# Second stage's down projection in seven block products, its weights' sums made in stage 1 and parked in device memory

## The chip, the cores and the metric

One core of a Trainium2 chip runs the whole kernel. The metric is device time in microseconds (us) of one execution. Engines are named as in the profile: PE (TensorE matmul), PEld (its weight load), DVE (VectorE), ACT (ScalarE), POOL (GpSimd), SP (SyncE, which issues nearly all DMAs here).

## The reference

Windowed attention, a gated feed-forward layer (stage 1) and a second feed-forward layer with a squared ReLU (stage 2). The change touches stage 2 and the preparation of its weights.

```python
attn = _attn_ref(q, k, v)                  # 4 x 8 heads, 576 tokens, window 64
x = heads side by side                     # 2304 tokens x 512
xn = x / rms(x) * rms_g                    # stage 1, d_ff = 1536
x = (silu(xn @ w_gate) * (xn @ w_val)) @ w_out
h = x @ w_in                               # stage 2, d_ff = 2048
out = (maximum(h, 0) ** 2) @ w_out2
```

## The kernel before

**Precision.** Every float32 operand of a product is kept as a high and a low part (`h`, `l`, type fp32r). A product of two of them is three matmuls for each 128 rows of contraction: high by high, low weight by high input, high weight by low input. The split of an operand is a cast on ACT or DVE (the high part) and a subtraction on DVE or POOL (the low part).

**Order.** Nothing is issued as it is written. `Schedule` collects steps, each with an engine (or two to choose from), a cost, the buffers that it reads and writes and a rank, and `issue` lays them out engine by engine in a simulated order; `LAG` is the delay that it assumes from a step's end to the start of a step on another engine. The engines then run their lists strictly in that order, with semaphores for the dependencies.

**Stage 1** (attention and the gated layer) decodes its weights on ACT and DVE (`decode`, L529 to L554). Beside it run 16 *jobs*, which prepare the weights of stage 2: `park_up(p)` and `park_down(p)` for each of 8 pairs p of 128-wide blocks of d_ff. A job decodes two blocks, splits them and writes them to device memory (`su`, `sd`). `park_up` also makes the four weight sums that the up projection's seven products need; `park_down` writes its two blocks as they are.

**Stage 2** works on 4 token blocks q of 576 tokens (two halves j of 288) and 8 pairs p, two pairs (`PG`) to a group. Tokens go in two halves of two q each (`HALVES`); in each half the 4 groups follow each other, and in a group the 2 token blocks. `operands(q)` makes the seven input blocks from `acc`. `up2` makes one unit (q, p): seven products of 6 matmuls of 128x128 weights by 288 columns (L766), taken from PSUM by copies (L771) and additions (L772), then the squared ReLU (L797) and the split (L804, L227). `down2` then makes, for each of 4 blocks c of 128 output columns and 2 halves j, one product over both pairs: 4 contraction blocks, 12 matmuls (`mm3`, L584, L586, L588). The running sum lies in `acc`: before the product ACT copies it into the PSUM bank (L823), after it ACT or DVE copies the bank back (L225).

```python
def down2(ds, acts, q, first, last):
    for c in range(KC):
        for j in range(2):
...
                if not first:
...
                    sc.add("act", c_act(PN), lambda b=b, pre=pre: nc.scalar.copy(ps[b][:, :PN], pre), ...)
                pe(12 * len(ds) // 2 * c_mm(PN), mm, ...)
```

The down weights have three buffers (`d0` to `d2`), the up weights two, the activations of two units six buffers of which four are in use.

## Time and profile before

| | |
|---|---|
| time, median of 3 runs | 939.1 us (938.45 to 939.8) |
| the profiled execution: time, span | 938.64 us, 936.9 us |
| busy, share of the span: PE, PEld | 98%, 92% |
| busy: DVE, ACT, POOL | 65%, 58%, 4% |
| granted TensorE clock, mean | 1.000 |
| stage 1's gated layer without attention, then stage 2 | about 125 to 551 us, 551 to 933 us |
| last matmul's end to the span's end | 3.6 us |

The time of an execution lies 1.7 us above its span. Busy shares are means over stages; PE's busy time holds its modelled pipeline, so a full row means that matmuls follow each other without a gap, not that the array is at its peak. Matmuls of 288 columns start one every 133 ns though each is shown with some 295 ns, since they overlap.

### The profile page before, as it was taken

How to read it: one execution, taken by the hardware profiler on the slowest of the kernel's cores; microseconds unless marked ns; L12 is line 12 of the kernel's file. 1: busy time of each engine (PE TensorE's matmuls, PEld its weight loads, DVE VectorE, ACT ScalarE, POOL GpSimd, SP SyncE). 2: the span in 40 equal slices, each digit the busy share in tenths (PEclk: the TensorE clock that was granted, in tenths of full speed). 3: DMA queues.
4: the chain of work that ended last, by engine and by line, in shares of the span. 5: the costliest groups of instructions: out<-in, count | busy, mean ns of one | idle time of the engine just before them, and what ended most of it. 6: DMA issues, size and time to landing. Idle time of an engine off the chain costs nothing.

```text
span 936.9 us, 17182 instructions
## 1 busy us (share of the span) xinstructions
PE 920.5 (98%) x6786; PEld 864.0 (92%) x6786; DVE 612.4 (65%) x1325; ACT 541.9 (58%) x1318; POOL 42.1 (4%) x48
## 2 busy tenths in 40 slices
PE   7989999999999999999999999999999999999998
PEld 6778899889988988988988999999999999999998
DVE  6999997789989978889996374333347333323340
ACT  5887884465565656565653364455567534555554
POOL 1000000001000101010211000000000000000000
PEclk9999999999999999999999999999999999999999
DMA  8664730334624523524646042242425352424212
GB/s 252 217 204 140 221 99 6 121 134 167 226 73 150 206 113 125 200 91 169 213 152 230 1 169 80 79 169 80 169 80 200 129 189 79 172 77 169 80 58 89
DMA packets 48001, 130.62 MB, mean 139 GB/s; under 512 B 5936, under 2 KB 22320, under 8 KB 43824
## 3 DMA queue, kind: packets, MB, share of 16 engines
q1 hardware_dynamic: 47392, 129.39, 40.0%
q8 instruction: 53, 0.87, 0.4%
q14 instruction: 28, 0.23, 0.1%
q10 hardware_dynamic: 528, 0.13, 0.1%
HBM read 101.71 MB, written 27.79 MB: 138 GB/s over the span
## 4 chain that ended last, share of the span: by engine, by line
PE 88%; DVE 9%; DMA 1%; ACT 0%; issue 0%; SPq 0%; DVEq 0%; ACTq 0%
PE ps L584 22%; PE ps L586 22%; PE ps L588 22%; PE ps L766 19%; DVE sm L422 2%; DVE R L226 1%; DMA k<-kT 1%; DVE xw L482 1%; PE ps L417 1%; PE ps L440 1%; DVE acc L445 1%; DVE Q L540 0%; DVE Q L539 0%; PE ps L907 0%; PE ps L430 0%; DVE pt L225 0%
## 5 line engine op out<-in xcount | busy, mean ns | idle before, releaser
L766 PE MATMUL ps<-R 128*128 128x288 f32 x1344 | 187.8, 295 | 0.0
L225 ACT COPY acc<-ps 128x288 f32<-128x288 f32 (+4 forms) x217 | 93.0, 431 | 160.3 <-PE ps L588 159.5
L766 PEld LDWEIGHTS ps<-R 128*128 128x128 f32 x1344 | 181.7, 188 | 0.1
L586 PE MATMUL ps<-L,R 128*128 128x288 f32 (+3 forms) x520 | 119.3, 322 | 0.0
L584 PE MATMUL ps<-L,R 128*128 128x288 f32 (+3 forms) x520 | 119.3, 322 | 0.0
L588 PE MATMUL ps<-L,R 128*128 128x288 f32 (+3 forms) x520 | 119.1, 321 | 0.0
L772 DVE TENSOR_TENSOR Q<-ps,Q 128x288 f32<-128x288 f32 x64 | 29.0, 454 | 117.6 <-ACT Q L771 106.7
L584 PE MATMUL ps<-R 128*128 128x256 f32 (+4 forms) x452 | 102.6, 347 | 0.8 <-ACT R L225 0.7
L586 PE MATMUL ps<-R 128*128 128x256 f32 (+4 forms) x452 | 100.5, 343 | 0.0
L588 PE MATMUL ps<-R 128*128 128x256 f32 (+4 forms) x452 | 100.3, 342 | 0.0
L797 DVE SCALAR_TENSOR_TENSOR Q<-Q 128x576 f32<-128x576 f32 x62 | 47.9, 773 | 72.3 <-ACT Q L771 71.3
L588 PEld LDWEIGHTS ps<-L,R 128*128 128x128 f32 x520 | 85.5, 188 | 4.2
L586 PEld LDWEIGHTS ps<-L,R 128*128 128x128 f32 x520 | 85.5, 188 | 4.2
L584 PEld LDWEIGHTS ps<-L,R 128*128 128x128 f32 x520 | 85.3, 188 | 4.2
L584 PEld LDWEIGHTS ps<-R 128*128 128x128 f32 x452 | 77.0, 188 | 9.0 <-ACT R L225 1.0
L586 PEld LDWEIGHTS ps<-R 128*128 128x128 f32 x452 | 77.4, 189 | 7.0
L588 PEld LDWEIGHTS ps<-R 128*128 128x128 f32 x452 | 77.4, 189 | 7.0
L771 ACT COPY Q<-ps 128x288 f32<-128x288 f32 x128 | 51.1, 400 | 46.0 <-PE ps L766 44.6
L225 ACT CAST L<-Q 128x512 fp32r<-128x512 f32 (+3 forms) x81 | 45.8, 573 | 54.8 <-DVE Q L627 50.3
L227 DVE TENSOR_TENSOR L<-Q,L 128x576 fp32r<-128x576 f32 (+2 forms) x90 | 66.0, 742 | 10.8 <-ACT L L804 9.8
L424 ACT ACTIVATE sm<-sm,nb 128x128 f32<-128x128 f32 (+1 forms) x144 | 55.7, 392 | 17.5 <-DVE nb L422 16.6
L657 ACT COPY ps<-acc 128x512 f32<-128x512 f32 (+2 forms) x101 | 55.1, 550 | 16.2 <-DVE acc L225 15.0
(105 smaller groups left out, 1471.6 us busy)
## 6 DMA issues: line engine op xcount, KB each, us to landing
Q<-w SPq DMA_DIRECT2D x68, 512.0 KB, 4.6
R<-su SPq DMA_DIRECT2D x16, 1792.0 KB, 7.2
su<-L SPq DMA_DIRECT2D x24, 512.0 KB, 4.6
R<-sd SPq DMA_DIRECT2D x11, 1024.0 KB, 5.2
v<-vw SPq DMA_DIRECT2D x36, 256.0 KB, 3.6
sd<-L SPq DMA_DIRECT2D x16, 512.0 KB, 5.3
L<-sd SPq DMA_DIRECT2D x5, 1024.0 KB, 4.9
q<-qT SPq DMA_DIRECT2D x36, 128.0 KB, 3.2
```

What stands on the lines that cost most here:

```text
L225: copy = lambda e, out, in_: nc.scalar.copy(out, in_) if e == "act" else nc.vector.tensor_copy(out, in_)
L227: two = lambda e, out, a, b, op: (nc.vector if e == "dve" else nc.gpsimd).tensor_tensor(out, a, b, op=op)
L422: at("dve", 0.21, lambda p=p, i=i_, j=j: nc.vector.tensor_tensor_reduce(out=T[sm][:, p, :nk], in0=s_ps[j][:, i, :nk], in1=T["mask"][:, P - ...
L424: at("act", 0.39, lambda p=p: nc.scalar.activation(T[sm][:, p, :nk], T[sm][:, p, :nk], AF.Exp, bias=T[nb][:, p : p + 1], scale=-1.0, accum ...
L584: nc.tensor.matmul(acc, wh, xh, start=(i == 0 and not seeded), stop=False, skip_group_check=seeded)
L586: nc.tensor.matmul(acc, wl, xh, start=False, stop=False, skip_group_check=seeded)
L588: nc.tensor.matmul(acc, wh, xl, start=False, stop=(i == n - 1), skip_group_check=seeded)
L657: add("act", c_act(n), lambda b=b, dst=dst: nc.scalar.copy(ps[b][:, :n], dst), r=keys("acc", c, t), w=[("ps", b)])
L766: nc.tensor.matmul(bank, w_, x_, start=(start and i == 0), stop=(i == len(terms) - 1), skip_group_check=True)
L771: take = lambda src, k, dst, kd: act(lambda: nc.scalar.copy(dst(), src), [k], [kd])
L772: plus = lambda src, k, other, s, j: sc.add("dve", c_dve(PN), lambda: nc.vector.tensor_tensor(e(s, j), src, T[other], op=ALU.add), r=[k, o ...
L797: nc.vector.scalar_tensor_tensor(T[s], T[s], 0.0, T[s], op0=ALU.max, op1=ALU.mult)
```

## The change

`down2` takes the form that `up2` has. Two blocks of output columns (of 128, from the two halves of 256), two blocks of d_ff rows and two token halves make a 2 by 2 block product, done as seven products and sums of weights and activations in place of eight. Two such chains (k = 0, 1) cover 512 output columns, each product over both pairs (6 matmuls). `park_down` now makes four weight sums and writes seven blocks, as `park_up` does (`park_pair`). `up2` makes, from the squared ReLU of its four blocks, three more differences (R1 to R4 with the in-place ones) and splits seven blocks in place of four, as two pieces of 5 and 2 blocks (1440 and 576 columns). The running sum is no longer copied into PSUM: VectorE adds the bank to `acc` in place. `operands` also makes its differences in place in `acc`. A load of weights comes in two parts, each waited for by itself; the down weights have two buffers, the activations one set of two (a second for the last block). The planner's assumed delay is 0.25 in place of 0.4 from the stage-1 jobs on, and the stage-1 weights lie in other slots (`PLACE`).

```diff
-PLACE = [1, 7, 8, 2, 3, 4, 5, 6, 0]
+PLACE = [5, 6, 7, 1, 2, 3, 4, 8, 0]
...
-            EXTRA[:] = 0.09, 0.1
+            EXTRA[:] = 0.09, 0.1, 0.25
...
-    make(dr, [NPAIR, P, 2, 2, WE], F32, "sd")
+    make(dr, [NPAIR, P, 2, 7 * 256], F32, "sd")
...
+    def park_pair(z, p, srcs, swap):
+        f = decode(srcs, after=closed2)
...
+        one(1, a21, a22, ALU.add, fk[2] + fk[3])
+        one(0, lambda: q(1), a11, ALU.subtract, [("q", 1)] + fk[0])
+        one(2, a11, a21, ALU.subtract, fk[0] + fk[2])
+        one(3, a12, lambda: q(0), ALU.subtract, [("q", 0)] + fk[1])
...
+        park(first, fk[0] + fk[1], 512, to(A11, 512), (z, p, A11))
+        park(lambda: q(0, 2), [("q", 0), ("q", 1)], 512, to(Q2, 512), (z, p, Q2))
+        park(lambda: q(2, 2), [("q", 2), ("q", 3)], 512, to(Q3, 512), (z, p, Q3))
+        park(a22, fk[3], 256, to(A22, 256), (z, p, A22))
...
-    def park_down(p):
-        f = decode([w4[2 * p + i] for i in range(2)], after=closed2)
-            park(lambda i=i: T[f][:, i * WE : (i + 1) * WE], [f], WE, T["sd"][p][:, i], ("sd", p, i))
+    park_down = lambda p: park_pair("sd", p, [w4[2 * p + i] for i in range(2)], True)
...
+        for i, keys_ in enumerate(((A11, Q2), (Q3, A22))):
...
+        def turn(r, d, i, j):
+
+            sc.add("dve", c_dve(n2), lambda: sub(a(*d), a(*i), a(*j)), r=ka(*i) + ka(*j), w=ka(*d))
+            split(r, 1, lambda: a(*d), ka(*d))
...
+        product(Q4, B22, pa, ka, False)
+        plus(pa, ka, 1)
+        square(0, 2)
         yield
         product(Q3, R3, pc, kc, False)
+        plus(pc, kc, 2)
+        square(2, 1)
+        dif(3, 1, 0, 2)
+        dif(1, 2, 3)
         yield
         product(A22, R4, pc, kc, False)
+        take(pc, kc, lambda: e(5), ek(5))
+        square(5, 1)
+        dif(6, 5, 1)
         yield
+        for i, (o, m) in enumerate(PIECES):
...
+            sc.add("act", c_act(m * PN), lambda z=z, o=o, m=m: nc.scalar.copy(z("h"), e(o, m)), r=ek(o, m), w=bk("h"))
+            sc.add(DP, c_dp(m * PN), lambda eng, z=z, o=o, m=m: two(eng, z("l"), e(o, m), z("h").bitcast(F32), ALU.subtract), r=ek(o, m) + bk("h"), w=bk("l"))
...
     def down2(ds, acts, q, first, last):
-                if not first:
-                    pre = T["acc"][:, c, t0 : t0 + PN]
-                    sc.add("act", c_act(PN), lambda b=b, pre=pre: nc.scalar.copy(ps[b][:, :PN], pre), r=tkeys("acc", c, t0, PN), w=[("ps", b)])
-                pe(12 * len(ds) // 2 * c_mm(PN), mm, r=list(ds) + [f"{n}{z}" for en in acts for n in en for z in "hl"], w=[("ps", b)])
...
+            product(A11, B11, pc, kc, True)
+            if first:
+                sc.add("act", c_act(PN, True), lambda: nc.scalar.copy(pa, pc), r=[kc], w=[ka])
+            else:
+                sc.add("dve", c_dve(PN), lambda: nc.vector.tensor_tensor(pa, pc, y(0, 0), op=ALU.add), r=[kc] + yk(0, 0), w=[ka])
+            yield
+            product(A12, B21, pa, ka, False)
+            plus(pa, ka, 0, 0, True)
+            done(0, 0)
+            yield
+            product(Q2, R2, pc, kc, False)
+            plus(pc, kc, 0, 1, first)
+            yield
+            product(Q1, R1, pa, ka, True)
+            plus(pa, ka, 1, 1, first)
+            yield
+            product(Q4, B22, pa, ka, False)
+            plus(pa, ka, 0, 1)
+            done(0, 1)
+            yield
+            product(Q3, R3, pc, kc, False)
+            plus(pc, kc, 1, 1)
+            done(1, 1)
+            yield
+            product(A22, R4, pc, kc, False)
+            plus(pc, kc, 1, 0, first)
+            done(1, 0)
+            yield
+
+        for _ in zip(*(chain(k, 4 + 2 * k, 5 + 2 * k) for k in range(2))):
+            pass
...
-    d_ring = Ring([view("d0", "R", NX + 28 * 256, 4 * WE), view("d1", "R", NX - 4 * WE, 4 * WE), view("d2", "L", 12 * 2 * PN, 4 * WE)])
+    u_ring, d_ring = Ring(["u1", "u0"]), Ring(["d0", "d1"])
```

What this makes of the engines' lists, at three places. In the rows `ps_64` to `ps_71` are the eight PSUM banks, `Q` holds stage 2's results of `up2`, `L`, `R` and `Q_5362` (a second life of `Q_2595`) hold split operands and weights.

PE, inside a down projection of stage 2. Before, a bank takes 12 matmuls (two rows each of high, low weight, low input), and a whole product of `up2` (L766) may stand between two banks:

```order
L584 MATMUL ps_71<-L,R 128x288 x2
L584 MATMUL ps_71<-L 128x288 x2
L586 MATMUL ps_71<-L,R 128x288 x2
L586 MATMUL ps_71<-L 128x288 x2
L588 MATMUL ps_71<-L,R 128x288 x2
L588 MATMUL ps_71<-L 128x288 x2
L766 MATMUL ps_66<-R 128x288 x6
```

Now the end of the second chain's first product (bank 71), one product of `up2` (L793), and the start of the first chain's second product, which adds onto what VectorE has put into bank 68:

```order
L857 MATMUL ps_71<-Q_5362,L 128x288
L857 MATMUL ps_71<-L,R 128x288
L857 MATMUL ps_71<-L 128x288
L793 MATMUL ps_66<-R 128x288 x6
L857 MATMUL ps_68<-L,R 128x288
L857 MATMUL ps_68<-Q_5362,L 128x288
```

Each product has 6 matmuls now, and 14 of them stand where 8 of 12 stood. The product into bank 68 waits for a VectorE instruction that reads bank 69.

DVE, in the same part of stage 2. Before there is nothing of the down projection, only `up2`'s additions, squares and low parts:

```order
L797 SCALAR_TENSOR_TENSOR Q<-Q 128x576
L227 TENSOR_TENSOR L<-Q,L 128x576 x2
L772 TENSOR_TENSOR Q<-ps_68,Q_2595 128x288
L797 SCALAR_TENSOR_TENSOR Q<-Q 128x576
L772 TENSOR_TENSOR Q<-ps_68,Q_2595 128x288
```

Now, for one token block and group, the addition onto bank 70, nine of the in-place additions into `acc`, and the low part of 1440 columns behind them:

```order
L876 TENSOR_TENSOR ps_70<-ps_71,acc 128x288
L224 TENSOR_TENSOR Q<-Q 128x288 x2
L865 TENSOR_TENSOR acc<-ps_69,acc 128x288
L865 TENSOR_TENSOR acc<-ps_71,acc 128x288
L865 TENSOR_TENSOR acc<-ps_68,acc 128x288
L865 TENSOR_TENSOR acc<-ps_70,acc 128x288
L865 TENSOR_TENSOR acc<-ps_69,acc 128x288
L865 TENSOR_TENSOR acc<-ps_68,acc 128x288
L865 TENSOR_TENSOR acc<-ps_70,acc 128x288
L865 TENSOR_TENSOR acc<-ps_71,acc 128x288
L865 TENSOR_TENSOR acc<-ps_69,acc 128x288
L225 TENSOR_TENSOR L<-Q,L 128x1440
```

Twelve VectorE instructions of the down projection came in, for each token block and group; ScalarE's copies into the banks are gone.

POOL, at the start of the jobs of stage 1, before (the first sums of the up weights, low parts of both kinds of block):

```order
L227 TENSOR_TENSOR Q_2595<-Q 128x256
L227 TENSOR_TENSOR L<-Q,L 128x512 x2
L227 TENSOR_TENSOR Q_2595<-Q 128x256
L227 TENSOR_TENSOR Q_2595<-Q,Q_2595 128x256
L227 TENSOR_TENSOR L<-Q,L 128x256
```

and now, where the sums of the down weights follow (the third to fifth row):

```order
L225 TENSOR_TENSOR Q_2595<-Q 128x256
L225 TENSOR_TENSOR L<-Q,L 128x512
L225 TENSOR_TENSOR L<-Q_2595,L 128x512
L225 TENSOR_TENSOR Q_2595<-Q 128x256 x2
L225 TENSOR_TENSOR Q_2595<-Q,Q_2595 128x256
```

POOL has 59 such instructions in stage 1 where it had 31, and 19 in stage 2 where it had 2.

## Rows read from the trace of the kernel before

**Rows 1.** The page: engines' busy time; PE, DVE, ACT and granted clock in 40 slices.
```profile
PE 920.5 (98%) x6786; PEld 864.0 (92%) x6786; DVE 612.4 (65%) x1325; ACT 541.9 (58%) x1318; POOL 42.1 (4%) x48
...
PE   7989999999999999999999999999999999999998
...
DVE  6999997789989978889996374333347333323340
ACT  5887884465565656565653364455567534555554
...
PEclk9999999999999999999999999999999999999999
```

**Rows 2.** PE's waits from 126 us to the end.
```profile
engine line waited for: us in total, times, longest us
PE ps L486 <- DVE R L226: 0.6, 1, 0.6
```

**Rows 3.** Chain that ended last, late in stage 2: start, us, what.
```profile
848.96 8.00 PE ps L766 x60
...
870.44 0.54 PE ps L584 x4
870.98 0.53 PE ps L586 x4
871.51 0.53 PE ps L588 x4
```

**Rows 4.** Windows: stretch, length, busy us (instructions) of each engine, clock, DMA share, GB/s.
```profile
core 0: us, PE busy (x) PEld busy (x) DVE busy (x) ACT busy (x) POOL busy (x), PEclk, DMA share, GB/s
...
175.00:500.00 325.00, 325.00 (x1562) 288.53 (x1561) 289.04 (x389) 190.43 (x310) 34.53 (x30) 1.00 0.46 159
500.00:550.00 50.00, 50.00 (x255) 46.11 (x254) 24.66 (x38) 23.17 (x43) 1.29 (x1) 1.00 0.27 103
```

**Rows 5.** Stage 2's groups, 551 to 937 us: DVE, then ACT; busy us, mean ns, idle before.
```profile
L797 DVE SCALAR_TENSOR_TENSOR Q<-Q 128x576 f32<-128x576 f32 x62 | 47.9, 773 | 72.3 <-ACT Q L771 71.3
L227 DVE TENSOR_TENSOR L<-Q,L 128x576 fp32r<-128x576 f32 x60 | 44.8, 754 | 10.5 <-ACT L L804 9.8
L772 DVE TENSOR_TENSOR Q<-ps,Q 128x288 f32<-128x288 f32 x64 | 29.0, 454 | 117.6 <-ACT Q L771 106.7 <-PE ps L766 10.4
L226 DVE TENSOR_TENSOR R<-acc,R 128x1152 fp32r<-128x1152 f32 x2 | 2.7, 1351 | 6.2 <-ACT R L726 6.2
...
L771 ACT COPY Q<-ps 128x288 f32<-128x288 f32 x127 | 50.7, 400 | 45.8 <-PE ps L766 44.4 <-DVE Q L772 1.2
L804 ACT CAST L<-Q 128x576 fp32r<-128x576 f32 x62 | 41.3, 676 | 8.9 <-DVE Q L797 8.6
L823 ACT COPY ps<-acc 128x288 f32<-128x288 f32 x96 | 38.8, 404 | 2.8
L771 ACT COPY ps<-ps 128x288 f32<-128x288 f32 x31 | 12.0, 388 | 10.7 <-PE ps L766 10.6
L726 ACT CAST R<-acc 128x1152 fp32r<-128x1152 f32 x2 | 2.3, 1168 | 0.0
```

**Rows 6.** Timeline in stage 2: start, us, engine, instruction, idle before it.
```profile
639.78 0.40 ACT L771 COPY Q<-ps 128x288 f32<-128x288 f32 x1 [0.28 <-PE ps L766]
640.22 0.76 DVE L797 SCALAR_TENSOR_TENSOR Q<-Q 128x576 f32<-128x576 f32 x1 [0.23 <-ACT Q L771]
...
644.33 1.76 PE L766 MATMUL ps<-R 128*128 128x288 f32 x12
...
645.32 0.40 ACT L771 COPY Q<-ps 128x288 f32<-128x288 f32 x1
```

**Rows 7.** Line L227 (low parts and weight sums), DVE and POOL: min/median/max ns.
```profile
L227 POOL TENSOR_TENSOR L<-Q,L x20: 742/1351/2229, 194.8 to 710.8; 128x512 fp32r<-128x512 f32 x14, 128x256 fp32r<-128x256 f32 x4, 128x576 fp32r<-128x576 f32 x2
...
L227 DVE TENSOR_TENSOR Q<-Q,Q x12: 410/420/1517, 194.5 to 488.6; 128x256 f32<-128x256 f32 x12
```

**Rows 8.** Timeline of DVE and POOL in stage 1 around one POOL instruction.
```profile
492.91 0.69 DVE L533 TENSOR_SCALAR Q<-Q 128x1024 uint32<-128x1024 uint32 x1
493.64 1.23 DVE L534 SCALAR_TENSOR_TENSOR Q<-Q 128x1024 uint32<-128x1024 uint32 x1
493.79 2.23 POOL L227 TENSOR_TENSOR L<-Q,L 128x512 fp32r<-128x512 f32 x1 [3.57 <-ACT L L225]
...
495.38 1.19 DVE L535 TENSOR_SCALAR Q<-Q 128x1024 uint32<-128x1024 uint32 x1
```

**Rows 9.** DMA issues: KB each, median us from issue to landing.
```profile
R<-su SPq DMA_DIRECT2D x16, 1792.0 KB, 7.2
...
R<-sd SPq DMA_DIRECT2D x11, 1024.0 KB, 5.2
```

More of the change, by code (lines that the diff above doesn't have):

```diff
@@ L54 @@
 class Schedule:
-    LAG = 0.4
     def __init__(self):
@@ new lines, in park_pair, with load @@
+        park(lambda: q(2, 2), [("q", 2), ("q", 3)], 512, to(Q3, 512), (z, p, Q3))
+        park(a22, fk[3], 256, to(A22, 256), (z, p, A22))
+    park_up = lambda p: park_pair("su", p, [w3[2 * p + i, 0] for i in range(2)], False)
+    park_down = lambda p: park_pair("sd", p, [w4[2 * p + i] for i in range(2)], True)
+    jobs = [j for p in range(NPAIR) for j in ((park_up, p), (park_down, p))]
+    PARTS = (0, 1024, 1792)
+    def load(ring, z, p):
+        u = ring.next()
+        for i, keys_ in enumerate(((A11, Q2), (Q3, A22))):
+            part = lambda t, i=i: t.rearrange("p (h n) -> p h n", h=2)[:, :, PARTS[i] : PARTS[i + 1]]
+            sc.add("sp", 3.4 - 0.8 * i, lambda i=i, part=part: nc.sync.dma_start(out=part(T[u].bitcast(F32)), in_=T[z][p][:, :, PARTS[i] : PARTS[i + 1]]), r=[(z, p, o) for o in keys_], w=[(u, i)], lag=2.5)
+        return u
@@ new lines, in operands, with unit @@
+        turn(R1, (0, 0), (0, 1), (0, 0))
+        turn(R3, (0, 1), (1, 1), (0, 1))
+        turn(R2, (1, 1), (1, 1), (0, 0))
+        turn(R4, (1, 0), (1, 0), (1, 1))
+        return x
+    PIECES = ((0, 5), (5, 2))
+    ORDER = (B11, R2, B22, R1, R3, B21, R4)
+    def unit(name, places):
+        off = iter(places)
+        for z in "hl":
+            for i, (o, n) in enumerate(PIECES):
+                t, at_ = next(off)
+                view(f"{name}{z}{i}", t, at_, n * PN)
+                for k in range(n):
+                    sc.names[name, z, ORDER[o + k]] = sc.names[f"{name}{z}{i}"][k * PN // G32 : (k + 1) * PN // G32]
+        return name
@@ L978, in attn_moe_moe2 @@
-    dn_ring.slots, dn_ring.i = [6, 7], 0
+    NB2 = 14 * 256
+    wblock("u0", "R", 56 * PN)
+    wblock("u1", "R", 56 * PN + NB2)
+    wblock("d0", "R", 56 * PN + 2 * NB2)
+    wblock("d1", "L", 14 * PN)
+    u_ring, d_ring = Ring(["u1", "u0"]), Ring(["d0", "d1"])
+    e_ring = Ring([view(f"e{i}", "Q", i * 7 * PN, 7 * PN) for i in range(2)])
+    sc.add("none", 0.001, close3, w=[(z, i) for z in ("Q2", "Q3") for i in range(NQ // G32)])
+    unit("b0", [("L", o * PN) for o in (0, 5, 7, 12)])
+    unit("b1", [("Q3", 0), ("Q3", 5 * PN), ("L", 14 * PN + NB2), ("Q3", 7 * PN)])
@@ L983, in begin @@
     def begin(h, g, q, i):
         if (h, g, i) not in us:
-            us[h, g, i] = load_up(g * PG + i)
-        if (h, g, 0) not in ds:
-            ds[h, g, 0] = load_down(g * PG)
+            us[h, g, i] = load(u_ring, "su", g * PG + i)
         if q not in xs:
             xs[q] = operands(q)
-        acts[g, q, i] = ("b6", "b7") if (h, g, q, i) == units[-1] else (b_ring.next(), b_ring.next())
-        return up2(us[h, g, i], xs[q], acts[g, q, i])
-    def after(h, g, q, i):
-        if i == 0 and (h, g, q) != units[-1][:3]:
-            flush()
-            for j in range(1, PG):
-                if (h, g, j) not in ds:
-                    ds[h, g, j] = load_down(g * PG + j)
+        return up2(us[h, g, i], xs[q], acts(h, g, q)[i])
@@ L999, in after, with products_done @@
+    def products_done(h, g, q, i):
+        if i == 0 and not final(h, g, q):
+            flush()
+            for j in range(PG):
+                if (h, g, j) not in ds:
+                    ds[h, g, j] = load(d_ring, "sd", g * PG + j)
+    def after(h, g, q, i):
         if i == PG - 1:
-            if (h, g, q, i) == units[-1]:
+            if final(h, g, q):
                 flush()
-            state["prev"] = lambda: down2([ds[h, g, j] for j in range(PG)], [acts[g, q, j] for j in range(PG)], q, g == 0, g == NPAIR // PG - 1)
+            state["prev"] = lambda: down2([ds[h, g, j] for j in range(PG)], acts(h, g, q), q, g == 0, g == NPAIR // PG - 1)
@@ L1004, in attn_moe_moe2, with end_of_unit @@
+    def end_of_unit(unit, run):
+        next(run)
+        products_done(*unit)
+        next(run, None)
+        after(*unit)
     prev = None
-    for unit in units + [None]:
-        run = unit and begin(*unit)
+    for unit_ in units + [None]:
+        run = unit_ and begin(*unit_)
         for k in range(3):
@@ L1012, in attn_moe_moe2 @@
         if prev:
-            next(prev[1], None)
-            after(*prev[0])
-        prev = run and (unit, run)
-        if unit == units[0]:
-            for _ in run:
-                pass
+            end_of_unit(*prev)
+        prev = run and (unit_, run)
+        if unit_ == units[0]:
+            for k in range(3):
+                next(run)
             clock[0] = max(c1, clock[0])
-            after(*unit)
+            end_of_unit(unit_, run)
             prev = None
```

192 lines of the change are left out of this document (89 added, 103 removed).

## The prediction

> **What bounds the kernel now.** I read the page first [rows 1]: PE is busy 98% of the span and its clock is at the top digit in every slice, while DVE shows 65%, ACT 58% and POOL 4%. A mean of 98% leaves open whether PE waits somewhere, so the waits come next: from 126 us to the end PE waits for 0.6 us in all, once [rows 2]. The chain that ended last says the same from the other side: in stage 2 it consists of PE instructions alone. It also gives the price of a matmul. 60 matmuls of 288 columns take 8.00 us, 133.3 ns each, and the 12 matmuls of one down product take 0.54 + 0.53 + 0.53 = 1.60 us, again 133.3 ns [rows 3]. So the number of matmuls sets the time of stage 2, at 133.3 ns apiece, as long as the other engines keep up. The windows then show where they have least to spare: between 175 and 500 us of stage 1 DVE is busy 289.0 of 325.0 us, between 500 and 550 us only 24.7 of 50 [rows 4].
>
> **What the change takes away.** The down projection has 4 token blocks by 4 groups, 16 rounds. A round was 8 products of 12 matmuls, 1536 in all; it becomes 14 products of 6, 1344 in all. The up projection keeps its matmuls and so does stage 1. That is 192 fewer, and 192 x 133.3 ns = **25.6 us**. The kernel's 96 ACT copies of `acc` into banks (38.8 us, 404 ns each [rows 5]) also go, but ACT did them beside a PE that did not wait, so I credit them with nothing.
>
> **What it adds in stage 2, as load.** Two units of `up2` and one `down2` make 28 products of 0.80 us, 22.4 us of PE. By the order, DVE has in that time: 16 instructions with a PSUM operand and 288 columns (2 onto a bank, 10 into `acc`, 4 in `up2`) at 0.454, 7.3 us; two copies of about 0.45, 0.9; for each unit one difference of 576 columns (about 0.76, from the 576-column rows) and two of 288 (at most 0.454), 3.3 in all; two low parts of 1440 columns. The trace has 0.754 us for 576 and 1.351 for 1152 [rows 5]; on that line 1440 is 1.65, twice 3.3. One small low part (0.75) and half a square (0.5) remain. The sum is 16.0 of 22.4 us, 72%. ACT has some 10 copies at 0.40, two casts of 1440 columns (0.676 at 576, 1.168 at 1152 [rows 5], so 1.41) and two of 576, and squares: about 13 us. Neither is a bound in the steady part.
>
> **As a chain.** New in kind is that PE's second product of a chain needs a DVE result that needs the first product. The timeline gives the handovers: a product's 12 matmuls start at 644.33, its last 6 end their slots at 645.13 (6 x 0.133 after the first 6), and the ACT copy behind that half starts at 645.32; so PE to the next engine takes 0.19 us. ACT to DVE takes 0.04 (640.18 to 640.22) [rows 6]. An addition with a PSUM result has no row. The nearest below is the ACT copy from PSUM to PSUM, 0.388, the nearest above the DVE addition out of PSUM, 0.454 [rows 5]; I take 0.454, the same engine. With some 0.1 us back to PE the chain is 0.19 + 0.454 + 0.1 = 0.75 us. The order puts the other chain's product and mostly one of `up2` between, 0.80 to 1.60 us. So it is hidden, with 0.05 us to spare at the worst place and 0.85 usually, **0 us**, if DVE takes up the addition at once. What may stand ahead of it on DVE's strict list is a 1440-column low part, 1.65 us. Behind the waiting addition stand the squares and low parts of the next units, which PE needs a period later.
>
> **Where the cover is thin.** Three places. The first period after stage 1 has the operands of a token block and a first `down2` without spare time: DVE is loaded to about 20 us of 23.4, ACT to about 22. At the start of the second token half two `operands` are made, each with 4 differences and the low parts, about 8.1 us of DVE; with two periods (32.0, less 6 x 0.454 that a first group leaves to copies) that is 45.5 us of DVE against 56 products, 44.8 us; over 84 products it is 64 of 67. A deficit of 0.7 us is partly covered by results made ahead. I take 1 us of stall for each of these two places, between 0 and 3.
>
> **In stage 1.** The sums of the down weights are new: by the order 13 more low parts and 14 more sums on DVE, 28 more instructions on POOL (59 for 31), 9 more casts on ACT. On DVE a sum of 256 columns is 0.42 [rows 7], a low part of 512 about 0.65 (between 0.42 at 256 and 0.754 at 576): 13 x 0.65 + 14 x 0.42 = 14.4, say 15 us. To this comes what POOL costs DVE. Beside a POOL low part of 2.23 us the decode step L535 took 1.19 us where the like step L533 took 0.69 with POOL quiet, 0.5 more [rows 8]; the 12 DVE sums have a median of 420 ns beside a minimum of 410, but one of 1517 [rows 7]. So a POOL instruction costs DVE between 0 and 0.5 us where it meets one; I take 0.3, 28 x 0.3 = 9. DVE in 175 to 500 us becomes 289 + 15 + 9 = 313 of 325 us, 97%, which still fits, with the half idle 500 to 550 us behind it for jobs that come late. PE's list of stage 1 changes only by 16 exchanged rows. I take 1 us of stall, between 0 and 3.
>
> The Trainium skill ("SBUF — State Buffer", section "SBUF: two separate sides") speaks against this change: the port pair that DVE and GpSimd share is an exclusive lock, held for the whole instruction, and the other engine blocks. It bears on the 0.3 us just taken; the slowed L535 and the 1517 ns sum agree with it in kind, the median of 420 ns shows that it seldom strikes. [...]
>
> **DMA.** A pair's down weights grow from 1024 to 1792 KB: four loads of 7.2 us [rows 9] for each group of two token blocks, 28.8 us of 44.8. With two buffers in place of three, the first parts (1024 KB, 5.2 us each [rows 9]) of a new group start when the old group's product with `Q1` is over and are wanted 19 products later: 10.4 us against 15.2. Hidden, 0 us; without that cover the delay would be a few us per group.
>
> **The sum.** 25.6 less 1 + 1 + 1 is 22.6. The profiled execution was 938.64 us with a span of 936.9, the median of the runs is 939.1, half a thousandth more; against the median the forecast is 939.1 - 22.6 = **916.5 us**. The 3.6 us after the last matmul stay: an addition and a copy out as before.
>
> **Rivals.**
> *Nothing stalls*: 939.1 - 25.6 = 913.5. For it: PE waited 0.6 us in 811 [rows 2], and the planner has laid the lists out with more distance than the chain needs. Against it: the three thin places.
> *DVE becomes the bound where it is fullest*: if each new POOL instruction costs DVE its whole length, 18 sums at 0.742 and 10 low parts at 1.351 [rows 7], that is 26.9 us, and DVE needs 289 + 15 + 27 = 331 of 325 us: 6 us of PE stall in stage 1, with 3 more at each thin place of stage 2, 921 to 928. [...] Against it: the median of 420 ns [rows 7], and the empty half of 500 to 550 us.
> *The down chains wait for DVE (slower)*: if DVE's additions regularly stand behind a low part of 1440 columns, PE waits up to 1.65 us; once in each of 16 rounds this costs 26.4 us, all of the gain, (939.9), twice 52.8 (966). It decides at 25.6 / 16 = 1.6 us of wait per round. For it: additions that were few and early (L772, 29.0 us) become 16 per round, and DVE's list is strict. Against it: DVE is idle 6 of 22 us, in the kernel before it idled 117.6 us ahead of L772 alone [rows 5], and two products stand between.
> *The matmuls saved do not show*, for weights come late or the removed work was not on PE's path: 937 to 941. Rows 2 and 9 speak against it.
>
> **How the numbers follow.** Likeliest, 914.5 to 920 around 916.5: 0.45. Nothing stalls, 912.5 to 914.5: 0.30. DVE bound in part, 920 to 928: 0.15. A gain eaten for the most part but not all, 0.03; no change, 0.02; chains that wait, slower: 0.05. The range from 912.8 to 924 leaves out about 0.03 below and 0.17 above. A measurement of this kernel can tell about 0.2% (1.9 us) from no change; so faster 0.93, same 0.02, slower 0.05.
>
> **What would show it.** PE's instructions should fall by 192 and stay back to back at 133.3 ns. The list of PE's waits should hold some 3 us in three places, led by DVE: an entry "down product waits for the addition onto a bank" of 10 us or more means the chain rival; PE waits between 175 and 550 us, with DVE near full there and POOL beside it, mean the port; waits for weights mean the DMA. The PSUM addition should read about 454 ns and the 1440-column low part 1.65 us. Wrong would make the prediction above all a DVE price: 0.1 us more on each of 256 additions of the down rounds is 1.6 us more DVE per round, still hidden, but 0.4 us more (16 x 0.4 = 6.4) would fill DVE.

## The result and the profile after

The changed kernel takes 926.25 us (925.82 to 926.65, 4 runs) beside 939.06 us (938.45 to 939.8); the ratio is 0.9863, with a 95% interval of 0.9846 to 0.988. It is faster by 12.8 us. The forecast was 916.5 us in a range of 912.8 to 924.0: the sign was right, the size was not, 9.8 us of the expected 22.6 did not come.

The page's totals and the slices of PE of the changed kernel answer to [rows 1]:

```profile
PE 901.9 (98%) x6594; PEld 841.7 (91%) x6594; DVE 743.6 (80%) x1575; ACT 574.7 (62%) x1294; POOL 105.6 (11%) x93
...
PE   7989999999999999999999999999999999999998
```

PE has 192 instructions fewer (6594 after 6786), as counted. On the page it still looks full. The list of its waits from 126 us on, which held one entry of 0.6 us [rows 2], shows what is new:

```profile
engine line waited for: us in total, times, longest us
PE ps L793 <- ACT ps L223: 2.6, 5, 0.8
PE ps L582 <- ACT ps L655: 2.2, 2, 1.3
PE ps L857 <- DVE L L225: 0.9, 1, 0.9
PE ps L857 <- DVE ps L876: 0.9, 1, 0.9
PE ps L793 <- DVE Q L798: 0.9, 1, 0.9
PE ps L484 <- DVE R L224: 0.7, 1, 0.7
```

The windows of the changed kernel (stretch, length, then busy time of PE, PEld, DVE, ACT and POOL, clock, DMA share, GB/s; the first two answer to [rows 4]) say where:

```profile
175.00:500.00 325.00, 322.80 (x1550) 286.24 (x1549) 297.98 (x399) 197.26 (x326) 61.44 (x55) 1.00 0.51 176
500.00:550.00 50.00, 50.00 (x248) 45.60 (x247) 30.25 (x45) 25.91 (x46) 4.27 (x4) 1.00 0.26 90
551.00:575.00 24.00, 23.86 (x170) 23.43 (x169) 18.24 (x32) 19.13 (x38) 4.45 (x2) 1.00 0.56 205
575.00:700.00 125.00, 124.08 (x928) 123.09 (x927) 83.53 (x148) 73.37 (x141) 9.62 (x6) 1.00 0.43 148
700.00:760.00 60.00, 56.40 (x418) 55.44 (x418) 50.27 (x85) 40.04 (x76) 9.95 (x5) 1.00 0.58 206
```

By busy time PE loses 2.2 us in stage 1, 0.9 us between 575 and 700 us, and 3.6 us at the start of the second token half.

**What a wait costs.** Two of these waits, with the work ahead of them, in the timeline of the changed kernel (start, us, engine, instruction, idle before it):

```profile
710.13 1.65 DVE L225 TENSOR_TENSOR L<-Q,Q 128x1440 fp32r<-128x1440 f32 x1
710.20 2.87 POOL L225 TENSOR_TENSOR Q<-Q,Q 128x576 fp32r<-128x576 f32 x1 [7.72 <-ACT Q L841]
...
711.70 1.98 DVE L224 TENSOR_TENSOR Q<-Q 128x576 f32<-128x576 f32 x1
...
713.61 0.75 DVE L224 TENSOR_TENSOR acc<-acc 128x576 f32<-128x576 f32 x1
714.28 0.45 DVE L876 TENSOR_TENSOR ps<-ps,acc 128x288 f32<-128x288 f32 x1
```
```profile
710.59 0.30 PE L857 MATMUL ps<-L,R 128*128 128x288 f32 x1
711.84 0.40 PE L857 MATMUL ps<-L 128*128 128x288 f32 x1 [0.94 <-DVE L L225]
712.08 0.30 PE L857 MATMUL ps<-L,R 128*128 128x288 f32 x1
...
714.78 0.40 PE L857 MATMUL ps<-L,R 128*128 128x288 f32 x1 [0.92 <-DVE ps L876]
```

From the matmul before the first wait to the one after it, 1.25 us pass (710.59 to 711.84) where 0.13 is the pitch, and the next one follows after 0.24 instead of 0.13. So a wait shown as 0.94 us costs 1.12 + 0.11 = 1.23 us: the list hides about 0.28 us of each, since a matmul is drawn 0.30 us long and starts every 0.13, and since the first one after a wait is slow. The ten waits of the list without L484 are 7.5 us; with 10 x 0.28 they are 10.3 us. The span fell by 936.9 - 924.5 = 12.4 us where 25.6 us of matmuls went, so 13.2 us were given back; the other 2.9 us are in waits too short for the list. By the starts of the matmuls 0.9 us of them lie in the first period of stage 2 (the 180 matmuls behind the last one of stage 1).

| place | cost with restarts, us, rounded | forecast |
|---|---|---|
| stage 1, two waits for L655 (1.3 and 0.9 us at 295.7 and 325.0 us) | 2.2 + 0.56 = 2.8 us | 1 |
| start of the second half, four waits (711.8, 714.8, 752.9 us, and at 736.6 us the fifth wait of the list's first row) | 3.6 + 1.1 = 4.7 us | 1 |
| four seed copies of `up2` (595.6, 618.7, 780.8, 803.8 us) | 4 x (0.46 + 0.28) = 3.0 us | 0 |
| the rest: first period of stage 2 (0.9 us, forecast 1) and short waits elsewhere | 2.9 us | 1 |

**The seed copies** are the place that the prediction did not look at. `up2`'s second product A12 needs ACT's copy of the first one's bank. In the timeline of the changed kernel:

```profile
593.30 1.96 ACT L841 CAST Q<-Q 128x1440 fp32r<-128x1440 f32 x2
...
595.16 0.39 ACT L223 COPY ps<-ps 128x288 f32<-128x288 f32 x1
...
595.61 1.58 PE L793 MATMUL ps<-R 128*128 128x288 f32 x10 [0.46 <-ACT ps L223]
```

ACT's list has both casts of a finished unit (1440 and 576 columns, 1.96 us) ahead of the copy. Between A11 and A12 stands one product of 0.80 us. The kernel before left all 32 of these copies to ACT. With the change the planner may give them to VectorE as well (`take` in `up2` went from ACT alone to either engine, which the section on the change does not list); in the changed kernel ACT still has 30 of them.

**Stage 1's waits.** The one at 295.7 us, followed back in the trace of the changed kernel. First SP's list (start, us, what), with its longest wait of this stretch (from 268 to 282 us), then the load's transfer in the chain (start, us), then ACT:

```profile
268.78 0.80 SPq L519 DMA_DIRECT2D Q<-w  x2
280.67 1.73 SPq L681 DMA_DIRECT2D su<-L  x2
...
283.72 0.60 SPq L519 DMA_DIRECT2D Q<-w  x1
```
```profile
SPq L681 <- POOL L L225: 11.1, 1, 11.1
```
```profile
283.72 7.74 DMA Q<-w
```
```profile
291.56 1.12 ACT L529 ACTIVATE Q<-Q 128x1024 f32<-128x1024 uint32 x1 [3.05 <-DMA Q<-w]
...
295.05 0.61 ACT L655 COPY ps<-acc 128x512 f32<-128x512 f32 x1
```

SP's queue has a store of a job (L681) ahead of the loads of the stage-1 weights, and stands 11.1 us with it, until POOL has made the low part that it stores. Then it issues three stores and two loads within 4 us. The load of 283.72 takes 7.74 us, where the median of the 68 of its kind is 4.7, so it is late twice: in its start and in its length. ACT stands 3.05 us on the decode that needs it, and the copy that PE's bank needs (L655) stands behind that. The wait at 325.0 us goes back in the chain to the same pair, a store (L681) at 317.46 and a load of 6.24 us behind it.

### The profile page after: what moved, and what is told of

The parts are those of the page before. It is cut to its first block, busy times and chain, and to the rows that moved or that the text cites. A ratio compares the mean times of both kernels' runs of the same rounds, so it can differ in the third digit from the quotient of the medians.

```text
span 924.5 us, 17383 instructions
## 1 busy us (share of the span) xinstructions
PE 901.9 (98%) x6594; PEld 841.7 (91%) x6594; DVE 743.6 (80%) x1575; ACT 574.7 (62%) x1294; POOL 105.6 (11%) x93
## 4 chain that ended last, share of the span: by engine, by line
PE 80%; DVE 13%; ACT 3%; DMA 2%; issue 1%; POOL 0%; SPq 0%; DVEq 0%; ACTq 0%; POOLq 0%
PE ps L857 19%; PE ps L793 17%; PE ps L582 13%; PE ps L584 13%; PE ps L586 13%; DVE sm L420 2%; DMA Q<-w 2%; DVE R L224 1%; ACT Q L841 1%; PE ps L415 1%; DVE xw L480 1%; PE ps L438 1%; DVE Q L538 1%; PE ps L428 1%; PE ps L988 1%
## 5 line engine op out<-in xcount | busy, mean ns | idle before, releaser
L793 PE MATMUL ps<-R 128*128 128x288 f32 x1344 | 188.9, 296 | 3.7 <-ACT ps L223 2.6
L793 PEld LDWEIGHTS ps<-R 128*128 128x128 f32 x1344 | 181.4, 188 | 6.1 <-ACT ps L223 4.5
L857 PE MATMUL ps<-L,R 128*128 128x288 f32 x630 | 169.9, 297 | 0.9 <-DVE ps L876 0.9
L857 PE MATMUL ps<-Q,L 128*128 128x288 f32 x480 | 133.4, 296 | 0.0
L857 PEld LDWEIGHTS ps<-L,R 128*128 128x128 f32 x630 | 118.4, 188 | 1.7 <-DVE ps L876 1.2
L865 DVE TENSOR_TENSOR acc<-ps,acc 128x288 f32<-128x288 f32 x136 | 61.6, 456 | 67.5 <-PE ps L857 67.2
L223 ACT COPY acc<-ps 128x288 f32<-128x288 f32 (+4 forms) x152 | 67.9, 452 | 55.6 <-PE ps L857 27.6
L582 PE MATMUL ps<-R 128*128 128x448 f32 (+3 forms) x436 | 99.0, 349 | 0.8 <-ACT R L223 0.7
L584 PE MATMUL ps<-R 128*128 128x448 f32 (+3 forms) x436 | 97.1, 344 | 0.0
L586 PE MATMUL ps<-R 128*128 128x448 f32 (+3 forms) x436 | 96.8, 344 | 0.0
L223 ACT CAST L<-Q 128x512 fp32r<-128x512 f32 (+3 forms) x93 | 52.5, 576 | 62.8 <-DVE Q L625 47.0
L857 PEld LDWEIGHTS ps<-Q,L 128*128 128x128 f32 x480 | 90.5, 189 | 0.0
L225 POOL TENSOR_TENSOR L<-Q,L 128x512 fp32r<-128x512 f32 (+2 forms) x39 | 55.2, 1416 | 273.9 <-ACT L L841 234.6
L841 ACT CAST L<-Q 128x1440 fp32r<-128x1440 f32 (+1 forms) x30 | 31.0, 1036 | 62.4 <-PE ps L857 62.1
L224 DVE TENSOR_TENSOR Q<-Q 128x288 f32<-128x288 f32 (+1 forms) x96 | 58.2, 606 | 12.4 <-ACT Q L806 9.8
L655 ACT COPY ps<-acc 128x512 f32<-128x512 f32 (+2 forms) x101 | 54.5, 548 | 14.6 <-DVE acc L223 13.1
L582 PE MATMUL ps<-L,R 128*128 128x512 f32 (+2 forms) x184 | 55.3, 371 | 2.2 <-ACT ps L655 2.2
```

Of the source, the lines that this page charges most:

```text
L223: copy = lambda e, out, in_: nc.scalar.copy(out, in_) if e == "act" else nc.vector.tensor_copy(out, in_)
L224: sub = lambda out, a, b: nc.vector.tensor_tensor(out, a, b, op=ALU.subtract)
L225: two = lambda e, out, a, b, op: (nc.vector if e == "dve" else nc.gpsimd).tensor_tensor(out, a, b, op=op)
L582: nc.tensor.matmul(acc, wh, xh, start=(i == 0 and not seeded), stop=False, skip_group_check=seeded)
L584: nc.tensor.matmul(acc, wl, xh, start=False, stop=False, skip_group_check=seeded)
L586: nc.tensor.matmul(acc, wh, xl, start=False, stop=(i == n - 1), skip_group_check=seeded)
```

## The experiments

Each was timed beside the kernel before, which had medians of 939.2, 939.74 and 939.23 us in the three groups of four. The changed kernel's 926.25 us, taken beside 939.06, is what they are held against; between groups, differences as small as 0.7 us are not told apart. How many matmuls PE starts in a stretch tells what it lost there, short waits included, at 0.133 us each.

**Stage 1: old jobs for the down weights.** The sums are not made.

```diff
+        if swap:
+            park(first_(T, f, 0), fk[0] + fk[1], 512, ..., (z, p, A11))
+            park(first_(T, f, 1), fk[2] + fk[3], 512, ..., (z, p, Q2))
+            return
```

> The changed kernel, but the jobs of the down weights do what they did before (two blocks of 512 written as they are, no sums); the second part of each down load takes up weights of the same size in place of the sums that are not made, so the output is not the reference's. Theory A (two waits of PE at 295.7 and 325.0 us, 2.75 us with their restarts, come from the added work of stage 1): 926.25 - 2.75 = 923.5 us, no PE wait above 0.2 us between 175 and 550 us. Rival (they come from the other slots of the stage-1 weights or from the planner's smaller delay, which both stay here): 926 us, with waits of the same size. Stage 2 keeps its 10 us of waits by both.

Measured: 924.72 us (924.4 to 927.29). One wait of stage 1 is left in the list (0.6 us, at 248 us), where there were two of 2.2 us. The profiled execution (924.4 us) is 1.9 us faster, which is what the waits say with their restarts, 2.8 less 0.9. So most of the stage-1 loss comes with the added work, but not all of it: with the old jobs, the new slots and the smaller delay a wait of 0.6 us stands where the kernel before had none.

**Stage 1: no POOL in the jobs.**

```diff
-        sc.add(DP, c_dp(n), lambda e: two(e, like(v(1)), ...
+        sc.add("dve", c_dve(n), lambda e="dve": two(e, like(v(1)), ...
-        one = lambda o, i, j, op, r: sc.add(DP, c_dp(256), lambda e: two(...
+        one = lambda o, i, j, op, r: sc.add("dve", c_dve(256), lambda e="dve": two(...
```

> The changed kernel, with all weight sums and low parts of the stage-1 jobs on VectorE (in the changed kernel POOL has 59 of them). Theory P (each POOL instruction costs VectorE about as much as VectorE would need for it): the busy time of VectorE between 175 and 500 us stays below 325 us, time 924 to 928 us. Rival D (POOL takes the work off VectorE at next to no cost): 59 x 0.55 = 32 us more for VectorE, 298 + 32 = 330 of 325 us, PE waits of 5 us or more in stage 1, 931 us or more.

Measured: 923.67 us (923.49 to 923.8), faster than the changed kernel by 2.6 us; PE has no wait in stage 1 after 175 us. Its windows:

```profile
175.00:500.00 325.00, 325.00 (x1565) 288.76 (x1565) 281.44 (x421) 198.06 (x329) 0.00 (x0) 1.00 0.48 164
500.00:550.00 50.00, 50.00 (x254) 45.94 (x254) 44.25 (x72) 32.80 (x59) 0.00 (x0) 1.00 0.45 150
```

VectorE does the work of 59 POOL instructions more, and its busy time falls, from 298.0 + 30.3 = 328.2 us to 281.4 + 44.3 = 325.7 us. It is not the same work otherwise: the planner also moved 18 casts, 7.2 us on VectorE, to ACT. ACT's largest group of casts from 175 to 550 us, in the changed kernel and without POOL in the jobs, has 11 of them:

```profile
L223 ACT CAST L<-Q 128x512 fp32r<-128x512 f32 x52 | 31.9, 619 | 30.0 <-DVE Q L625 14.4 <-DMA sd<-L 5.8 <-DMA su<-L 5.2
```
```profile
L223 ACT CAST L<-Q 128x512 fp32r<-128x512 f32 x63 | 38.3, 619 | 29.7 <-DVE Q L625 15.3 <-DMA su<-L 9.7 <-DMA sd<-L 3.5
```

What POOL costs is therefore read form by form. The groups of VectorE from 175 to 550 us (busy us, mean ns, idle before), first the changed kernel:

```profile
L530 DVE TENSOR_SCALAR Q<-Q 128x1024 f32<-128x1024 f32 x27 | 22.2, 821 | 5.5 <-ACT Q L527 5.5
L225 DVE TENSOR_TENSOR Q<-Q,Q 128x256 f32<-128x256 f32 x20 | 13.0, 648 | 0.1
L625 DVE TENSOR_TENSOR Q<-ps,Q 128x448 f32<-128x448 f32 x20 | 12.4, 621 | 5.8 <-PE ps L586 5.5
```

and without POOL in the jobs:

```profile
L530 DVE TENSOR_SCALAR Q<-Q 128x1024 f32<-128x1024 f32 x27 | 18.6, 687 | 4.1 <-ACT Q L527 4.1
L225 DVE TENSOR_TENSOR Q<-Q,Q 128x256 f32<-128x256 f32 x32 | 13.3, 417 | 0.0
L625 DVE TENSOR_TENSOR Q<-ps,Q 128x448 f32<-128x448 f32 x20 | 12.5, 624 | 10.4 <-PE ps L586 9.0 <-ACT Q L527 1.1
```

Most forms of VectorE whose operands all lie in SBUF are longer in the mean with POOL at work, 821 for 687 and 648 for 417 ns, but not all (L538 takes 1220 ns in both, L532 1222 and 1220); those that read PSUM are not (621 and 624). Summed over all groups (count times mean above the mean without POOL), POOL costs VectorE 27.6 us in the changed kernel, 0.47 us for each of its 59 instructions, and 15.7 us in the kernel before, 0.51 us for each of 31. Both sums come from some 20 rows each. VectorE itself needs 29.2 us for the 59 (17 low parts at 0.683, 42 others at about 0.42). So POOL relieves it of next to nothing in stage 1. That the waits of stage 1 went for this reason alone is not shown, since ACT's and VectorE's lists changed with it.

**The same in the kernel before** (the same two edits there):

> The kernel before, with the 31 weight sums and low parts of its stage-1 jobs that POOL has given to VectorE. Theory P (a POOL instruction costs VectorE 0.5 us, about what VectorE needs for it): VectorE's busy time between 175 and 550 us stays within 4 us of 289.0 + 24.7 = 313.7 us, and the time stays at 939 us, since PE does not wait either way. Rival (POOL costs VectorE 0.3 us or less): VectorE's busy time there grows by 31 x (0.55 - 0.3) = 8 us or more.

Measured: 939.21 us (938.41 to 941.17, 10 runs), ratio 1.0002 (0.9992 to 1.0011), no wait of PE after 126 us beyond the 0.6 us of L486. VectorE's windows:

```profile
175.00:500.00 325.00, 325.00 (x1565) 288.77 (x1564) 278.91 (x399) 196.92 (x325) 0.00 (x0) 1.00 0.46 158
500.00:550.00 50.00, 50.00 (x253) 45.95 (x252) 27.51 (x40) 24.46 (x45) 0.00 (x0) 1.00 0.28 107
```

278.9 + 27.5 = 306.4 us, 7.3 less than the 313.7 us with POOL [rows 4]. Theory P allowed 4 us either way, so its number failed. But here too casts moved: ACT has 52 and 9 of the two forms of 512 columns where it had 41 and 5, and these 15 are 6.3 us of VectorE's time at 0.42. Form by form VectorE needs 16.7 us for the 31 instructions, and POOL cost it about 15.6. So P's reading of a POOL instruction stands: it relieved VectorE of about 1 us in all, without effect on the time, since PE did not wait for VectorE.

**Stage 1: stores later in SP's list.**

```diff
-        sc.add(DP, c_dp(n), ..., r=keys_ + [g], w=[g])
+        sc.add(DP, c_dp(n), ..., r=keys_ + [g], w=[g], lag=5.0)
```

> The changed kernel in which the planner takes 5.0 us in place of 0.25 from a job's low part to what follows it, so that the store to device memory comes later in SP's list. Theory Q (the two waits of stage 1 arise in SP's queue: a store that waits for a stretched low part stands ahead of the load of a stage-1 weight): both waits go, 923.5 us, VectorE busy as before (298 of 325 us). Rival P (VectorE and POOL beside each other make the weights late whatever SP does): waits of 2 us or more remain, 925 to 927 us.

Measured: 937.06 us (935.87 to 938.02, 8 runs). The two waits are gone from stage 1, but the jobs came late as a whole (VectorE is busy 47.0 us between 500 and 550 us, and 275.7 between 175 and 500), and at the start of stage 2 PE waits for them:

```profile
PE ps L793 <- ACT Q L223: 7.7, 2, 5.6
```

So this run does not separate the SP queue from VectorE. That a store ahead of the load is the link is read from the trace of the changed kernel; no run tests it by itself.

**Stage 2: no POOL for the low parts.**

```diff
-            sc.add(DP, c_dp(m * PN), lambda eng, z=z, ...
+            sc.add("dve", c_dve(m * PN), lambda eng="dve", z=z, ...
```

> The changed kernel, with the low parts of stage 2's activations made by VectorE alone (in the changed kernel POOL makes 19 of them). Theory P (a POOL instruction stretches the VectorE instruction beside it, 0.75 to 1.98 us at 711.7): the start of the second token half loses 1.2 us at each of two places less, about 924 us. Rival D (VectorE is simply full there, 22.7 of 25 us between 700 and 725 us, and POOL takes work off it): 19 x 0.75 = 14 us more VectorE work in stage 2, 1.5 to 3 us of it at that place, 927 to 929 us.

Measured: 928.08 us (926.31 to 929.73), not clearly different from 926.25. From 700 to 760 us PE loses 2.4 us instead of 3.6. L224, which took 1.98 us at 711.70, takes 0.75 there, and the wait for L876 behind it is gone; the other three waits are shorter, but a new one of 1.1 us for an ACT copy stands at 714.84. The waits for seed copies became eight of 3.3 us in place of five of 2.6. So P holds for the stretched instruction. The time lies in D's range, but what D gives for it, 14 us more VectorE work, did not come as busy time (253.7 us from 551 to 910 us, 252.4 with POOL): VectorE got back 5 us of stretched instructions, most of it in L224 on 576 columns (32 of 757 ns where they were 909), and gave copies and squares to ACT. In stage 2 POOL thus does relieve VectorE, 14 us of work for some 5.

**Stage 2: no operands in the second half.** The second half reads those of the first.

```diff
-            xs[q] = operands(q)
+            xs[q] = operands(q) if h == 0 else xs[q - npr // HALVES]
```

> The changed kernel without the operands of the second token half (the products there read the operands of the first half again; not the reference's output). Theory O (four waits of 4.7 us in all between 711 and 753 us come from the 16 us of VectorE work for these operands): they go, 921.5 us. Rival (the lists of that place are tight without them): at least 2 us of waits remain between 700 and 760 us, 924 us or more.

Measured: 922.56 us (922.04 to 924.53), 3.7 us less; all of PE's waits from 700 to 760 us are gone. So the operands set them off. Whether it is their load or the lists that the planner makes of it, the next runs tell.

**The planner's assumed delay.** Only the number changes: 0.4, as before the change; 0.19, the handover from PE to ACT of [rows 6]; 0.10, further down, without POOL in the jobs.

```diff
-            EXTRA[:] = 0.09, 0.1, 0.25
+            EXTRA[:] = 0.09, 0.1, 0.4
```

> The changed kernel with the planner's assumed delay between engines at 0.4 in place of 0.25 us, as it was before. Theory L (the waits of stage 2 stand where the planner's list puts a short instruction that PE needs behind long ones, since it plans for too small a delay): more distance, the four waits of 0.7 us for the seed copies and part of the 4.7 us at the start of the second half go, 921 to 923 us. Rival (the lists lose the same for want of room whatever the assumed delay): 925 to 928 us.

Measured: 932.86 us (932.69 to 935.58), 6.6 us slower than at 0.25. The wait for seed copies, in PE's list:

```profile
PE ps L793 <- ACT ps L223: 6.6, 12, 1.5
```

More assumed delay did not give more distance. In ACT's list both casts (from 593.18 us, 1.96 us) stand ahead of the seed copy (595.05), as in the changed kernel, and the list has twelve such waits. A likely reading is that the planner holds the copy for not ready longer than it is and fills ACT with casts meanwhile. Theory L fell.

> The changed kernel with the planner's assumed delay at 0.19 us, the delay from PE to ACT read in rows 6. Theory S (four waits of 0.7 us stand where ACT's list has both casts of a unit, 1.96 us, ahead of the seed copy that PE needs; with 0.4 there were twelve such waits): with 0.19 the copy stands between the casts or ahead of them, at most two such waits, 922 to 924.5 us. Rival (the lists come out differently but as tight): 925 to 928 us with as many waits.

Measured: 921.61 us (920.6 to 922.11). No wait for a seed copy is left in PE's list, and none from 700 to 760 us. The window there, of this kernel, against 56.40 and 50.27 us of PE and VectorE in the changed kernel:

```profile
700.00:760.00 60.00, 60.00 (x450) 59.67 (x449) 50.74 (x90) 43.27 (x84) 7.07 (x4) 1.00 0.64 213
```

VectorE does as much (50.7 of 60 us), operands included, and PE does not wait: 450 matmuls for 418, 4.3 us. So the 4.7 us were not lack of room on VectorE: they came from lists in which one product's seed or low part stood behind long instructions. The delay changes more than the order, though. It also decides which engine takes a step: VectorE makes 11 of the 32 seed copies here, 2 in the changed kernel (groups from 551 to 925 us, first the changed kernel):

```profile
L223 DVE COPY ps<-ps 128x288 f32<-128x288 f32 x2 | 0.9, 458 | 0.0
```
```profile
L223 DVE COPY ps<-ps 128x288 f32<-128x288 f32 x11 | 5.1, 463 | 1.9 <-PE ps L793 1.9
```

And the seed copies are not free of waits; these have become too short for the list. One of six like it, in the timeline with the delay of 0.19:

```profile
660.43 1.40 ACT L841 CAST Q<-Q 128x1440 fp32r<-128x1440 f32 x1 [0.29 <-DVE Q L224]
...
661.74 0.40 ACT L223 COPY ps<-ps 128x288 f32<-128x288 f32 x1
...
662.18 0.96 PEld L793 LDWEIGHTS ps<-R 128*128 128x128 f32 x7 [0.32 <-ACT ps L223]
```

One cast is still ahead of the copy, where there were two. PE's matmuls start at 661.81, 662.18 and 662.42 us, which costs about 0.35 us, 2.1 us for the six. Between 575 and 700 and between 760 and 900 us PE starts 931 and 1042 matmuls where the changed kernel had 928 and 1040: 0.7 of the 3.0 us came back. So most of what the delay of 0.19 saves is the start of the second half. Theory S is right on the place of the copy; the 3 us that it counts for it came back by less than a quarter. Stage 1 keeps two waits of 1.7 us, at other places (459 and 506 us).

**ACT's second cast planned later.** All other delays stay.

```diff
-        dif(6, 5, 1)
+        dif(6, 5, 1, lag=0.9)
```

> The changed kernel, planned with 0.9 us in place of 0.25 from the last difference of a unit to its second cast alone, so that ACT's list has the seed copy of a later unit ahead of that cast where both stood before it; every other assumed delay stays. Theory S (the four waits of 0.7 us come from this order on ACT): they go, 926.25 - 2.9 = 923.3 us, and the waits at the start of the second half may stay. Rival (the waits come from the short room of the up projection's own chain, one product of 0.80 us, and return at other places): 925.5 to 927.5 us.

Measured: 925.91 us (924.73 to 927.58). The four waits are gone (PE loses 0.2 us from 551 to 700 us, 1.06 us in the changed kernel), the one at 736.6 and others of the second half stay, and a new one of 0.4 us stands at 897 us. Here, too, VectorE got more of the seed copies (9 of 32 for 2), so the run is not one of ACT's order alone. In the total little is left. Between 575 and 700 and between 760 and 900 us PE starts 932 and 1043 matmuls, 7 more than in the changed kernel, so about 0.9 of the 3 us came back. Between 700 and 760 us it starts 407 for 418, which takes 1.5 us again; most of that is TensorE's clock in the profiled execution (927.58 us), told below. The one execution with a mean clock of 1.000 took 924.73 us. S is right on the four waits of the list; that their 3 us return in the total is not shown.

**Together: no POOL in the jobs, delay 0.19.**

> No POOL in the jobs of stage 1 (923.67 us alone) and the assumed delay of 0.19 us together. If their savings lie in different places and add: 923.67 less what the delay of 0.19 saves, 920 to 922 us. Rival (with another delay stage 1's lists change too and take it back): 924 us or more.

Measured: 919.75 us (919.05 to 920.06), ratio to the kernel before 0.9788 (0.9773 to 0.9803). The savings nearly add (2.6 + 4.6 = 7.2): it beats the changed kernel by 6.5 us and the kernel before by 20.0. PE's list of waits from 126 us on is down to

```profile
PE ps L484 <- DVE R L224: 0.6, 1, 0.6
PE ps L857 <- ACT ps L874: 0.2, 1, 0.2
```

The span is 917.8 us; 936.9 - 25.6 = 911.3 would be all of the matmuls' gain, so 6.5 us remain: 0.8 us by which its stage 1 runs later from the start (the same matmul of it at 262.3 us and, in the kernel before, at 261.5 us; that is not the change, since the kernel without any POOL instruction, next, has it at 261.5), the row of L874, and waits too short for the list, six of them for seed copies.

> The changed kernel without POOL in the jobs and in stage 2, with the assumed delay of 0.19 us. If POOL costs VectorE as much in stage 2 as it takes off it, and the lists are no tighter: 919 to 920.5 us, as with POOL in stage 2 (919.75). Rival (VectorE is short of time in stage 2, most of all between 700 and 775 us, where it was busy 60.3 us): 921.5 us or more.

Measured: 919.93 us (919.54 to 921.41), the same. Without any POOL instruction in these stages VectorE is enough. That POOL costs it as much in stage 2 as it takes off it does not follow: the planner gave 11 copies to ACT with it, and form by form the 12 POOL instructions cost VectorE 1.4 us for 9 us of work.

> The changed kernel without POOL in the jobs, with the assumed delay of 0.10 us, under every handover that the trace shows. Theory (the lists follow the assumed delay, and it has its best where it is near the real 0.19 us): PE waits come back, 921 to 924 us. Rival (the smaller the better): 919.5 us or less.

Measured: 927.41 us (925.9 to 927.87). PE waits in many small pieces, as would follow if the planner takes results for ready that are not: nine times for L223 (1.6 us in all) and for L874, L876 and others. Without POOL in the jobs 0.25, 0.19 and 0.10 give 923.67, 919.75 and 927.41 us.

## Why the prediction was right and wrong

- **The matmuls: right.** 192 fewer at 133 ns. The runs with few waits come near the whole of it: 20.0 of 25.6 us with the delay of 0.19 and no POOL in the jobs.
- **Removed ACT work hidden: nothing speaks against it.** No run gained more than 20.0 of the matmuls' 25.6 us, so none shows a gain from the 96 copies; no run took them away alone.
- **Durations: right.** L876, the addition into PSUM, is 461 ns (0.454 taken), L865 456 ns, the low part of 1440 columns 1648 to 1658 ns (1.65). The groups of the changed kernel from 551 us on:

```profile
L225 DVE TENSOR_TENSOR L<-Q,L 128x1440 fp32r<-128x1440 f32 x15 | 24.7, 1648 | 0.0
...
L876 DVE TENSOR_TENSOR ps<-ps,acc 128x288 f32<-128x288 f32 x24 | 11.1, 461 | 6.9 <-PE ps L857 6.9
```

- **The down chains hidden: right.** One wait of 0.9 us for L876. The rival of the slower side did not come. The handover of 0.19 us is read rightly, though the six matmuls that end at 645.13 are the first of that row, not the last. The loads of stage 2 were hidden as well: none stands in PE's list.
- **"I take 1 us of stall" for each of three thin places: the step that failed**, in the sum of the stalls, and with it the claim that the rest is hidden. In their place the runs showed 2.8 us in stage 1, 4.7 at the start of the second half and 0.9 in the first period, and a fourth place of 3.0 us, the seed copies, was not in the sum; some 2 us more lie in short waits, 13.2 in all for 3. The step judged by load (VectorE at 313 of 325 us in stage 1, 45.5 us for 44.8 in the second half). VectorE was 92% in stage 1 and there were waits; it was busy 84% and 85% of the time from 700 to 760 us both in the changed kernel, with 3.6 us of waits, and with the delay of 0.19, with none. The load is a condition, since without the operands the waits go. But with the same load other lists have none of them: what decided was which engine had a few instructions, and what stood ahead of them.
- **"As a chain": worked out for the down projection only.** The same sum for `up2` (A11, ACT's copy, A12) is 0.19 + 0.39 + 0.1 = 0.68 us with one product of 0.80 us to hide it, and 1.96 us of casts on ACT's list that may come ahead. It needed no new number: the copy is in [rows 5] (388 ns), the handover in [rows 6], the casts in the prediction's own load (1.41 us for 1440 columns).
- **"A POOL instruction costs DVE between 0 and 0.5 us, I take 0.3": mis-sized, 0.5 measured.** The step rested on a median of 420 ns [rows 7]. The mean of the same twelve sums in the kernel before, in the groups of VectorE, was there to be read:

```profile
L227 DVE TENSOR_TENSOR Q<-Q,Q 128x256 f32<-128x256 f32 x12 | 8.6, 715 | 0.0
```

  715 for 420: a few that meet POOL pay a lot. The new instructions cost 27.6 - 15.7 = 12 us, not 9, and in stage 1 POOL takes next to no load off VectorE. Another term of the same sum was too large: of the 16 new low parts POOL got 10, so VectorE got 6 (36 for 30 between 175 and 550 us), not 13. VectorE came to 298.0 us, not 313.
- **The rival "DVE becomes the bound"** gave 921 to 928 and holds the time, in part by luck: it asked for 6 us of stall in stage 1, where 2.8 came, and the 3.0 us of the seed copies are not in it. Its mechanism holds only in part: the stage-1 loss goes away without POOL, as it says, while VectorE was not full (298.0 of 325 us), and 4.3 us of stage 2's loss go away with other lists at the same load. The Trainium skill ("SBUF — State Buffer", section "SBUF: two separate sides") has the shared port locked for a whole instruction; the 0.47 to 0.51 us for each POOL instruction are in the mean about half of such an instruction's own 0.74 to 1.35 us [rows 7], so in the mean it is not the whole length. The same section names as colliding a VectorE instruction with two SBUF inputs or in a fast mode that takes both port pairs; the unchanged 621 ns of L625, which has one of its inputs in PSUM, agrees.

## What to carry to other kernels

Price what POOL costs VectorE by the mean over the shortest of each form, before giving it work: in stage 1 here 59 instructions on POOL cost VectorE 27.6 us and saved it 29.2, and the kernel without them (and with 18 casts on ScalarE instead) was faster by 2.6 us; in stage 2 POOL's 19 instructions cost it some 5 us and saved it 14. Such a balance needs the count of every form on every engine, since a planner moves other work along. A busy share of 84% says little on waits where engines run strict lists: for every chain from PE over another engine back to PE, put the longest instructions that may stand ahead of its link against the products between. Of the delays tried for the planner, the handover that the trace shows, 0.19 us here, did best; 0.4 and 0.25, or 0.10, gave worse lists. And a list of waits without an entry is not a PE without loss: count the matmuls of the stretch too.
